# Score products in two column halves, then whole: two 64-column products become one of 128

## The chip, the core and the metric

The kernel runs on one core of a Trainium2 chip. The core has five engines that work through their own instruction queues and meet at semaphores: TensorE (PE, matrix products; its weight loads are listed apart as PEld), VectorE (DVE), ScalarE (ACT), GpSimd (POOL) and SyncE (SP, which here issues most DMAs). The metric is the device time of one execution in microseconds.

## What is computed

Thresholded attention over 8 batches of 8 heads, 576 positions and 64 numbers a head, followed by a gated MLP with a product over positions. Cut to what matters:

```python
scores = scale * np.matmul(q, k.transpose(0, 1, 3, 2))          # 576 x 576 for each head
thresh = np.max(scores, axis=-1, keepdims=True) - tau
scores = np.where(scores >= thresh, scores, -1000000000.0)
scores = scores - np.max(scores, axis=-1, keepdims=True)
attn = np.exp(scores)
attn = attn / (np.sum(attn, axis=-1, keepdims=True) + 1e-09)
x = np.matmul(attn, v)                                           # heads are then put side by side

h = np.maximum(x @ w_in, 0.0)
u, v = h[..., :512], h[..., 512:]
v_n = (v - mean(v)) / np.sqrt(var(v) + 1e-06)
v_s = np.einsum('ts,bsd->btd', w_spatial, v_n) + b_spatial[None, :, None]
out = (u * v_s) @ w_out
```

## The kernel before

Two heads are handled as a pair: head 0 of the pair lies in partitions 0 to 63 of a tile `qkT`, head 1 in 64 to 127, for q and for k, turned so that the 64 numbers of a head lie along the partitions. There are 32 pairs. The 576 rows of scores of a pair are cut into four chunks of 128 (c = 0 to 3) and a remainder of 64 rows; the remainders of two pairs that follow each other share a chunk of their own (c = 4). So every even pair has four steps and every odd pair five, 144 steps in all, 18 for each of the 8 batches. The list `steps` names the pair and the chunk of each step g.

A step computes the scores of 128 rows (for both heads, 576 columns each) in fp32 into one of two PSUM buffers, `s_ring[g % 2]`. A buffer spans three PSUM banks of 512 fp32 columns: head 0's scores start at column 96, head 1's at 864 (`at = (96, 864)`). Head 0 thus fills the rest of bank 0 (its first 416 columns, `cut`) and 160 columns of bank 1, head 1 fills 160 columns of bank 1 and 416 of bank 2. The two heads' products use different row halves of the array[...]. `part` (line 810) issues one stretch of columns of one head, as two products with 64 columns of weights each (k = 0 and 1), one for each half of the 128 score rows. In steps with c = 4 the two halves belong to two different pairs and so have different operands.

`scores` (line 823) issues three stretches: head 0's 160 columns in bank 1, head 1's 416 in bank 2, head 0's 416 in bank 0. `scores_end` (line 834) issues the last, head 1's 160 in bank 1. Both heads write bank 1 at different times, so `turn_bank` (line 829) puts an empty instruction on GpSimd, ScalarE or VectorE that waits for head 0's product in bank 1, and head 1's product waits for that.

After a step, `top` (line 840) takes the maximum over each head's 576 columns on VectorE (line 850), `shift` (line 856) makes the threshold's offset, ScalarE passes over each head (`spread`, lines 871 and 874), which frees the score buffer, and either ScalarE (`exps`, line 909) or VectorE (`keep` and `pick`, lines 893 and 902) turns the result into numerators. A DMA transposes them (`turn_p`, line 914), and TensorE multiplies them with v (lines 491 to 510). Two score buffers mean that step g + 2 begins once the passes of step g are done.

The order is written out by hand. For each batch a string of tokens is walked through, `S7:0` for `scores` of the batch's step 7, `G7`, `Y7` for `turn_bank` and `scores_end`, `M`, `B`, `E`, `F` for the maximum, the offset and the two passes, `Z`, `C`, `A` for the numerators, `T` for the transposing DMA, `P` for the product with v. Between them stand the tokens of the MLP (lines 627 to 767), the turning of q and k by TensorE (lines 434 and 453) and the loads (SyncE). Every engine works through its instructions in the order of this list. Between `S` and `Y` of one step no other TensorE work is listed as a rule, and nearly always other TensorE products, with weights of 128 by 128, lie between one step and the next.

The line numbers in the profile are those of the code printed here.

Of the kernel before, what the change touches and what calls it, by code (L numbers as in the profile page):

```python
# [184 lines left out]
def kernel(  # L185
# [18 lines left out]
    B, H, S, D = q.shape  # L204
# [5 lines left out]
    P = 128  # L210
# [15 lines left out]
    s_ring = [ps_s.tile([P, 1536], F32, name=f"s{i}") for i in range(2)]  # L226
# [147 lines left out]
    def shape_bias(_):  # L374


        for n in range(3):
            part = wsb[:, :, S + n]
            nc.gpsimd.tensor_copy(out=part, in_=bias)
            if n < 2:  # L380
                nc.gpsimd.tensor_tensor(out=bias, in0=bias, in1=part, op=ALU.subtract)
# [17 lines left out]
    qks, xns, xts = {}, {}, {}  # L399
# [86 lines left out]
    halves = [slice(64 * k, 64 * k + 64) for k in range(2)]  # L486
# [303 lines left out]
    at = (96, 864)  # L790
# [11 lines left out]
    def follow(b, a):  # L802

        tc.add_manual_dep(b.ins, a.ins.name, mybir.DependencyInfo(
            mybir.DependencyClass.Sync, mybir.DependencyReason.DATA), reason="shared bank")

    cut = 512 - at[0]
    opened, turned = {}, {}

    def part(g, h, lo, hi):  # L810

        i, c = steps[g]
        made = []
        for k in range(2):
            n, m = (i, 64 + c * P + 64 * k) if c < 4 else (i - 1 + k, S)
            made.append(nc.tensor.matmul(  # L816
                out=s_ring[g % 2][halves[k], at[h] + lo:at[h] + hi],
                lhsT=qks[n][halves[h], 0, m:m + 64],
                rhs=qks[n][halves[h], 1, 64 * (1 - h) + lo:64 * (1 - h) + hi],
                start=True, stop=True))  # L820
        return made

    def scores(g):

        opened[g] = part(g, 0, cut, S)[1]
        part(g, 1, S - cut, S)
        part(g, 0, 0, cut)

    def turn_bank(g, eng):

# [2 lines left out]

    def scores_end(g):

        follow(part(g, 1, 0, S - cut)[0], turned[g])

    negm = {}

# [255 lines left out]
    def run_token(tok, it):  # L1095
# [19 lines left out]
        m = 2 * b + a[0] if a else 0  # L1115
        if kind in "SGYMHKEFBZWCAT":
            {"S": scores, "G": lambda g: turn_bank(g, relay), "Y": scores_end, "M": top, "E": lambda g: spread(g, 0),
             "F": lambda g: spread(g, 1), "H": lambda g: top(g, slice(0, 1)),
             "K": lambda g: top(g, slice(1, 2)), "B": shift, "Z": exps, "W": mask, "C": keep, "A": pick, "T": turn_p}[kind](g)
# [124 lines left out]
```

## Time and profile before

| what | us |
|---|---|
| median of three runs (lowest to highest) | 434.66 (434.51 to 435.89) |
| the profiled execution's own time | 435.42 |
| its span, first to last instruction | 433.6 |
| score products, first to last start | 6.2 to 396.0 |
| MATMUL records of line 816 (two for each product) | 2304, 171.4 us busy |
| maximum, line 850 | 144 times 1.36 |
| passes of ScalarE, lines 871 and 874 | 288 times 0.74 |
| DMA | 88.15 MB, mean 203 GB/s |

The granted TensorE clock is full in every slice. A line of the timeline has the start, the length, the engine, the line of the code, the operation, the tile written and the tiles read, the shape of the array used by TensorE (rows*columns of weights, as in 64*64), the shape of one operand, how many instructions were merged, and in brackets the idle time before and what ended it. The starts of TensorE's records are observed, their ends are modelled.

### The profile page before, as it was taken

The page shows a single profiled execution, that of the slowest core. Times are in us where ns is not written, and L with a number is a line of the kernel's source. Part 1 is how long each engine was busy: PE and PEld are TensorE (multiplying, and loading weights), DVE is VectorE, ACT ScalarE, POOL GpSimd, SP SyncE. Part 2 cuts the span into 40 slices and gives each one's busy share as a digit, 9 for nine tenths or more (in the row PEclk, how much of TensorE's full clock was granted, in tenths as well). Part 3 has the DMA queues.
Part 4 walks back from the last instruction along what each step waited for, and adds up shares of the span by engine and source line. Part 5 has one row for each costly group of instructions (what it writes and reads, how often), then busy time and mean ns, then how long its engine had stood idle before and what let it go on. Part 6 is the DMA issues. An engine that isn't in the chain of part 4 may idle for free.

```text
span 433.6 us, 12917 instructions
## 1 busy us (share of the span) xinstructions
PE 407.3 (94%) x5028; PEld 253.7 (58%) x5028; DVE 374.6 (86%) x681; ACT 383.9 (89%) x587; POOL 167.5 (39%) x374
## 2 busy tenths in 40 slices
PE   7678879989999999998999999999999999999995
PEld 4446655565755666574665656555666656564642
DVE  6999989898989889987889988988999999998652
ACT  4999989999999988998988999999999989999262
POOL 1253525682335611545143713356114630264020
PEclk9999999999999999999999999999999999999999
DMA  7999999999899998999979999999999999889923
GB/s 195 224 237 232 246 247 221 194 212 197 226 241 212 246 208 183 218 184 178 254 139 250 216 159 248 233 209 205 232 209 232 181 232 194 172 124 193 164 68 118
DMA packets 224700, 88.15 MB, mean 203 GB/s; under 512 B 195648, under 2 KB 220352, under 8 KB 224640
## 3 DMA queue, kind: packets, MB, share of 16 engines
q1 hardware_dynamic: 224192, 86.75, 99.7%
q8 instruction: 39, 0.64, 0.6%
q10 hardware_dynamic: 368, 0.33, 0.2%
q0 software_dynamic: 80, 0.26, 0.2%
q14 instruction: 21, 0.17, 0.2%
HBM read 32.79 MB, written 9.44 MB: 97 GB/s over the span
## 4 chain that ended last, share of the span: by engine, by line
PE 64%; ACT 13%; DVE 8%; DMA 6%; issue 4%; POOL 3%; SPq 0%; ACTq 0%; DVEq 0%; POOLq 0%
PE s L816 26%; ACT e L874 6%; PE f L738 6%; DVE s L850 5%; PE f L496 5%; PE f L709 5%; PE f L434 4%; PE f L642 4%; PE f L767 4%; DMA pT<-p 3%; ACT p L909 2%; DMA xT<-xn 2%; ACT e L871 2%; PE f L491 2%; PE f L627 1%
## 5 line engine op out<-in xcount | busy, mean ns | idle before, releaser
L850 DVE TENSOR_REDUCE s<-s 128x2 f32<-128x1152 f32 x144 | 196.1, 1362 | 21.3 <-PE s L816 18.0
L816 PE MATMUL s<-qkT 64*64 64x160 f32 (+1 forms) x2304 | 171.4, 415 | 12.6 <-ACT e L874 6.6
L816 PEld LDWEIGHTS s<-qkT 64*64 64x64 f32 x2304 | 106.5, 131 | 71.3 <-ACT e L874 18.8
L874 ACT ACTIVATE e<-s,negm 128x576 f32<-128x576 f32 x192 | 133.1, 744 | 9.6 <-DVE negm L856 7.0
L909 ACT ACTIVATE p<-e 128x1152 f16<-128x1152 f32 x96 | 111.6, 1173 | 0.7 <-PE s L816 0.2
L871 ACT ACTIVATE e<-s,negm 128x576 f16<-128x576 f32 x96 | 66.8, 746 | 5.0 <-DVE negm L856 2.9
L320 POOL CAST v<-vl 128x512 bf16<-128x512 f32 x32 | 20.2, 631 | 77.0 <-PE s L816 65.7
L496 PE MATMUL f<-v,pT 128*128 128x65 bf16 x984 | 44.4, 194 | 0.0
L496 PEld LDWEIGHTS <-pT 128*128 128x128 f16 x1024 | 41.8, 98 | 2.2 <-issue 0.2
L293 POOL COPY qn<-ql 128x512 f32<-128x512 f32 x31 | 20.4, 659 | 49.9 <-PE s L816 47.5
L902 DVE TENSOR_TENSOR p<-e 128x576 int32<-128x576 int32 x48 | 37.2, 778 | 0.4 <-PE s L816 0.2
L738 PE MATMUL f<-wsT,vn 128*128 128x512 bf16 x135 | 33.0, 380 | 0.0
L491 PE MATMUL f<-v,pT 128*128 128x130 bf16 x123 | 27.3, 222 | 3.6 <-DMA pT<-p 3.5
L709 PE MATMUL f<-xT,w_in 128*128 128x512 bf16 x116 | 29.7, 380 | 0.5 <-ACT qkT L414 0.3
L694 POOL TENSOR_SCALAR vn<-vrel,rs,nm 128x512 bf16<-128x512 f32 (+1 forms) x35 | 28.1, 801 | 3.6
L642 PE MATMUL f<-w_in,xT 128*128 128x512 bf16 x112 | 27.9, 380 | 0.3 <-DMA xT<-xn 0.3
L446 POOL COPY qkT<-qkT 64x64 f32<-64x64 f32 x32 | 9.5, 296 | 44.8 <-PE s L816 17.6
L534 DVE TENSOR_TENSOR xn<-f,r 128x384 bf16<-128x384 f32 x46 | 24.9, 551 | 1.3 <-PE s L816 0.8
L856 DVE TENSOR_SCALAR negm<-s 128x2 f32<-128x2 f32 x144 | 22.2, 154 | 4.0 <-PE s L816 1.5
L767 PE MATMUL f<-w_o,gT 128*128 128x512 bf16 x100 | 25.4, 379 | 0.1
L893 DVE TENSOR_SCALAR e<-e 128x1152 uint16<-128x1152 f16 x48 | 23.0, 478 | 0.1
L687 POOL TENSOR_TENSOR rs<-rs,mhalf 128x1 f32<-128x1 f32 (+1 forms) x35 | 21.2, 607 | 2.9
(171 smaller groups left out, 531.4 us busy)
## 6 DMA issues: line engine op xcount, KB each, us to landing
vl<-in_v_dram SPq DMA_DIRECT2D x16, 512.0 KB, 5.3
ql<-in_q_dram SPq DMA_DIRECT2D x15, 512.0 KB, 4.6
kl<-in_k_dram SPq DMA_DIRECT2D x15, 512.0 KB, 5.3
out_dram<-oo SPq DMA_DIRECT2D x12, 512.0 KB, 3.7
pT<-p SPq DMA_TRANSPOSE x141, 4.6
uT<-in_moe_w_in_dram SPq DMA_DIRECT2D x3, 512.0 KB, 5.1
uT<-in_moe_w_spatial_dram SPq DMA_DIRECT2D x2, 576.0 KB, 4.4
vx<-in_v_dram SPq DMA_DIRECT2D x16, 64.0 KB, 4.3
```

The costliest lines, as they stand in the source:

```text
L491: nc.tensor.matmul(out=t[:, at:at + 130], lhsT=pt[:, 4, rows], rhs=vt[:, 4:6, :].rearrange("p b d -> p (b d)"), start=True, stop=False)
L496: nc.tensor.matmul(out=t[:, at + 65 * h:at + 65 * h + 65], lhsT=pt[:, 5 * h + j, rows], rhs=vt[:, 6 * h + j, :], start=False, stop=(h == 1 ...
L642: nc.tensor.matmul(out=t, lhsT=x_of(b, f, slice(c * P, (c + 1) * P)), rhs=w_in[:, f, 512:1024], start=(f == 0), stop=(f == 3))
L709: nc.tensor.matmul(out=t, lhsT=w_in[:, m, f * P:(f + 1) * P], rhs=x_of(b, m, slice(0, 512)), start=(m == 0), stop=(m == 3))
L738: nc.tensor.matmul(out=t, lhsT=vn[:, c, f * P:(f + 1) * P], rhs=wsT[:, c, 0:512], start=(c == 0), stop=(c == 4))
L767: nc.tensor.matmul(out=t[:n], lhsT=gs[b][:, f, c * P:c * P + n], rhs=w_o[:, f, :], start=(f == 0), stop=(f == 3))
L816: made.append(nc.tensor.matmul(out=s_ring[g % 2][halves[k], at[h] + lo:at[h] + hi], lhsT=qks[n][halves[h], 0, m:m + 64], rhs=qks[n][halves ...
L850: nc.vector.tensor_reduce(out=nm[:, heads], in_=view(s_ring[g % 2], at[h0], dims), axis=AX.X, op=ALU.max, negate=True)
L871: nc.scalar.activation(out=half_e(g)[0][:, S * h:S * h + S], in_=s, func=ACT.Exp, bias=bias_, scale=scale if steps[g][1] == 4 else 1.0)
L874: nc.scalar.activation(out=e, in_=s, func=ACT.Prelu, bias=bias_, scale=scale if steps[g][1] == 4 else 1.0, alpha=1e30)
L902: nc.vector.tensor_tensor(out=numerators(g).bitcast(I32), in0=e.bitcast(I32), in1=kept.bitcast(I32), op=ALU.bitwise_and)
L909: nc.scalar.activation(out=numerators(g), in_=e_ring[g % 3].rearrange("p h s -> p (h s)"), func=ACT.Exp)
```

## The change

`part` gets a flag `whole`. Where it is set and c < 4, one product with all 128 columns of weights (64 rows by 128 columns of the array) writes all 128 score rows, in place of two with 64 columns each. It is set for the second stretch of each head: head 0's 416 columns and head 1's last 160. The first stretch of each head, and all steps with c = 4, stay as they are.

```diff
-    def part(g, h, lo, hi):
+    def part(g, h, lo, hi, whole=False):
 
         i, c = steps[g]
+        whole = whole and c < 4
         made = []
-        for k in range(2):
+        for k in range(1 if whole else 2):
             n, m = (i, 64 + c * P + 64 * k) if c < 4 else (i - 1 + k, S)
             made.append(nc.tensor.matmul(
-                out=s_ring[g % 2][halves[k], at[h] + lo:at[h] + hi],
-                lhsT=qks[n][halves[h], 0, m:m + 64],
+                out=s_ring[g % 2][slice(0, P) if whole else halves[k], at[h] + lo:at[h] + hi],
+                lhsT=qks[n][halves[h], 0, m:m + (P if whole else 64)],
                 rhs=qks[n][halves[h], 1, 64 * (1 - h) + lo:64 * (1 - h) + hi],
                 start=True, stop=True))
         return made
...
-        part(g, 0, 0, cut)
+        part(g, 0, 0, cut, True)
...
-        follow(part(g, 1, 0, S - cut)[0], turned[g])
+        follow(part(g, 1, 0, S - cut, True)[0], turned[g])
```

## The prediction

> **What bounds the kernel now.** I began with the page: busy shares and the strip of 40 slices.
>
> ```profile
> PE 407.3 (94%) x5028; PEld 253.7 (58%) x5028; DVE 374.6 (86%) x681; ACT 383.9 (89%) x587; POOL 167.5 (39%) x374
> ...
> PE   7678879989999999998999999999999999999995
> ...
> PE 64%; ACT 13%; DVE 8%; DMA 6%; issue 4%; POOL 3%; SPq 0%; ACTq 0%; DVEq 0%; POOLq 0%
> PE s L816 26%; ACT e L874 6%; PE f L738 6%; DVE s L850 5%; PE f L496 5%; PE f L709 5%; PE f L434 4%; PE f L642 4%; PE f L767 4%; DMA pT<-p 3%; ACT p L909 2%; DMA xT<-xn 2%; ACT e L871 2%; PE f L491 2%; PE f L627 1%
> ```
>
> TensorE carries 64% of the chain of waits, and line 816, the one that is changed, 26% alone. Because a share is a mean over stages, I cut the span by stage (columns: stretch, its length, then PE, PEld, DVE, ACT, POOL busy):
>
> ```profile
> 6.20:100.00 93.80, 78.66 (x1049) 52.07 (x1052) 84.68 (x141) 87.01 (x130) 45.41 (x93) 1.00 1.13 228
> 100.00:397.00 297.00, 292.53 (x3650) 182.65 (x3647) 266.52 (x471) 278.07 (x424) 117.86 (x269) 1.00 1.04 205
> ```
>
> From 100 to 397 us PE lacks only 4.5 us of being always busy: what PE loses there, the kernel loses. From 6.2 to 100 it sits idle for 15.1 us, and the chain there runs through other engines too: 12.23 PE, 13.56 DVE, 15.22 ACT, and again. All 144 score steps lie in these two stretches; 38 begin before 100 us, 106 after. (DMA shows 9 in nearly every slice, a second full resource, but one that only gains room if the rest is slower.)
>
> **One step as it is.** The timeline around one step, then two pieces of the chain in order of time:
>
> ```profile
> 204.37 0.60 PE L434 MATMUL f<-identf,kn 128*128 128x128 f32 x4
> 204.90 0.91 PEld L816 LDWEIGHTS s<-qkT 64*64 64x64 f32 x16 [0.17 <-issue]
> 204.90 1.20 PE L816 MATMUL s<-qkT 64*64 64x160 f32 x16
> 206.03 0.14 PEld L453 LDWEIGHTS f<-identf,rl 128*128 128x128 f32 x1 [0.23 <-ACT qkT L416]
> 206.03 0.33 PE L453 MATMUL f<-identf,rl 128*128 128x128 f32 x1
> ```
>
> ```profile
> 204.97 1.13 PE s L816 x12
> ...
> 361.02 2.10 PE s L816 x24
> ```
>
> A step costs PE 1.13 us from its first weight load to the next work's. What is in it comes from the forms of line 816 (busy, mean ns):
>
> ```profile
> L816 PE MATMUL s<-qkT 64*64 64x416 f32 x1152 | 167.8, 521 | 0.0
> L816 PE MATMUL s<-qkT 64*64 64x160 f32 x1152 | 132.1, 308 | 12.6 <-ACT e L874 6.6 <-ACT e L871 3.9 <-DVE negm L856 1.5
> ```
>
> Each product is two records. 521 - 308 = 213 ns for 256 columns more is 0.83 ns a column, so 416 columns stream in 346 ns and 160 in 133; the rest of a record (shortest 296, less 133) is 163 ns of tail. Head 0 uses the upper 64 rows of the array, head 1 the lower 64, and they run side by side: head 0 streams 160 then 416, head 1 416 then 160. Each half needs 2 x 133 + 2 x 346 = 958 ns. Single records show it: from the step's start, head 1's second 416 record starts at 0.42 us, but head 0's 416 already at 0.325, in the array's other half. 0.96 plus about 0.05 exposed load plus the tail's part that the next work waits for makes 1.13.
>
> **What a change of shape costs.** Before the step runs a 128*128 shape. PE L434 ends at 204.97 by the record, and the first 64*64 load starts at 204.90, 0.07 before that end. Inside one shape loads go far ahead:
>
> ```profile
> 208.50 0.66 PE L434 MATMUL f<-identf,qn 128*128 128x128 f32 x4
> 208.89 0.64 PEld L709 LDWEIGHTS <-w_in 128*128 128x128 bf16 x4
> ...
> 244.27 0.41 PE L496 MATMUL f<-v,pT 128*128 128x65 bf16 x8
> 244.62 0.11 PEld L504 LDWEIGHTS <-pT 128*64 128x64 f16 x2
> ```
>
> L709 loads 0.27 us before L434's end (both 128*128); L504, where only the columns change (128*128 to 128*64), again waits until 0.06 before it. I went through the single records of all 301 changes of shape in this trace, of six kinds (128*128, 128*64, 64*64, each to each other): the earliest load is 0.073 us before the modelled end of the last product, never earlier; and in the 65 changes whose load waits for no semaphore it is 0.071 or 0.072 each time, never later. So a change of shape by itself makes the load wait until the array is empty. Price: after a 160-column record the next load starts 0.224 us after that record's start, and 0.05 more of load is exposed (first records 348 ns against 296), where 0.133 would do within a shape: 0.224 + 0.052 - 0.133 = **0.14 us**.
>
> **The change, part by part.**
>
> *Removed:* in steps with c < 4 the second pair of products becomes two instead of four. c = 4 occurs once in every odd pair, 16 of 144 steps; 128 steps change, and 128 x 4 = 512 records of each kind go (5028 to 4516). They streamed beside each other, so this frees no streaming time: 128 columns of weights take the same 0.83 ns per moving column. Line 434's fp32 records with 128*128 say so: 273 ns for 128 columns is 107 plus 166. At most the few ns between twin records go, 6.5 ns a step, 0.8 us in all.
>
> *Added:* a change of shape inside the step, 64*64 to 64*128. No row has it. Lower bound: nothing, if the upper half simply goes on. Upper bound, by the rows above: the whole array empties. I take the upper one, since all six kinds of change do that. The Trainium skill speaks against this change too: "TensorEngine Tiling (Array Packing)", Key Properties, says that changing the tiling mode, unlike changing the tile, drains TensorE. The page has no price; the trace has. Then, from the step's start: head 1's second 416 record starts at 0.42 and ends at 0.42 + 0.51 = 0.93; the first 64*128 load may start at 0.93 - 0.07 = 0.86. Head 0's 416 columns, which began at 0.325, begin now: second record at 0.86 + 0.05 + 0.35 = 1.26, end 1.26 + 0.51 = 1.77, next shape's load at 1.70. Head 1's 160 run beside it and end by 1.36. **1.70 - 1.13 = 0.57 us a step.** The same from the parts: 2 x 346 + 2 x 346 streamed one after the other is 1384 in place of 958, 0.43, plus one change at 0.14.
>
> Here a second rule could matter. "TensorE: Matmul & The Clock Gate", LDWEIGHTS, prices a weight load by its columns, 1/1.2 ns each, so 128 columns load 53 ns longer than 64, which the emptied array would expose: 128 x 0.053 = 6.8 us more. The row says less: after a change, line 453's fp32 load of 128 columns lengthens its product from 273 to 328 ns, 55, against 52 for 64 columns. I take the row (0.4 us in all) and keep 6.8 for the top of the range.
>
> 128 x 0.57 = 73 us. Seven steps start 0.77 to 1.1 us after the step before, overlapping it (the 2.10 us for two above, against 2 x 1.13): now 64*128 to 64*64 lies between and stops that, 7 x 0.16 = 1.1. Sum **74 us of PE work**.
>
> *Moved:* the relay (line 831), an empty instruction on POOL, ACT or DVE that tells head 1's last product that head 0 has left the shared bank, still waits for the same 64*64 product, ending at 0.49 after the step's start. Its follower could go at 0.61 before and at 0.86 now, so 0.25 us of cover come on top; that costs nothing. The DVE maximum (1.36), and behind it ACT's two passes (1.38), start 0.57 later; from 100 us on they had waited in PE's shadow, DVE 30 and ACT 19 us idle, and get more room. No DMA is issued or moved.
>
> *What absorbs it:* PE's idle, 15.1 + 4.5 = 19.6 us at most. From 8 to 35 us the chain goes PE 1.25, DVE 1.38, ACT 1.38 around the two score buffers, 4.4 us for two steps, so only every second step's 0.57 is on it: some six of twelve are hidden, 3.4 us. Of the 8.2 us idle between 30 and 100, and of the 4.5 after, I take half: 4 and 2. About 10 in all (chosen; ends 0 and 19.6).
>
> Sum against the profiled execution: 435.42 (span 433.6 plus 1.8 around it) + 74 - 10 = 499. That run lies 0.76 above the median of the three shown, 434.66; from the median **498 us**.
>
> **The rivals.**
>
> *Only the changed half waits (8%).* 64*128 over the upper rows might wait for head 0 alone. Its last 160 record starts at 0.195, so its load comes at 0.195 + 0.224 = 0.42 and its columns stream from 0.47 in place of 0.325, and the step ends 0.14 later: 128 x 0.14 = 18, a third absorbed, 447 us. For: no change in this trace leaves an untouched half running, so none shows what happens to it. Against: the page says the engine drains, and every record here waits for the last product of all.
>
> *The halves stop running side by side in 64*128 (5%).* Then head 1's 2 x 133 come after head 0: 128 x 0.27 = 34 more, 532 us. For: no 64*128 row. Against: 64*64 halves overlap fully.
>
> *No drain, no loss (5%).* Row split unchanged, so 64*128 could follow at 0.325 as now; half as many loads in that part, 0.8 us gained, 434 us, not slower. It decides if the change costs under about 0.01 us a step (128 x 0.01 = 1.3 us, which 0.3% of the time is). Against: the column-only change at 244.62.
>
> *It does not take effect (under 1%):* the new flag reaches `slice(0, P)` for every c < 4.
>
> **How the numbers follow.** Array emptied: 82%. Its own range is 434.66 + 74 - 20 = 489 to 434.66 + 74 + 6.8 = 515. The other cases lie far from it and are left out; I round the range to 485 to 515, with room below for a step that is 0.03 us cheaper than worked out. 0.3%, 1.3 us, is about what can be told from no change. Slower holds the first three cases, 95%; the no-loss case splits into 2% same and 3% faster.
>
> **What would show it.** Line 816 with 512 records 64*128; in a step, the first 64*128 load some 0.86 us after the first 64*64 load and 0.07 before the recorded end of head 1's 416; pieces of 1.70 in place of 1.13 in the chain; PE near always busy from 35 us on; DVE and ACT shares down by a tenth. A first 64*128 load at 0.42 or 0.19 would make it wrong, as would head 1's 160 beginning after head 0's 416.

## The result, and the profile after

The kernel after takes 1.149 times as long as the kernel before (95% interval 1.143 to 1.155). Its median of six runs is 504.79 us against 435.5 us for the kernel before beside it; three of the six ran longer than the rest (508 to 518 us), and this ratio, like those below, leaves such runs out; the other three took 500.35, 500.43 and 501.5 us. The profiled execution took 500.43 us, with a span of 498.7.

From the page of the kernel after, busy time, the strip for TensorE and the chain that ended last:

```profile
PE 481.9 (97%) x4469; PEld 224.1 (45%) x4516; DVE 377.6 (76%) x681; ACT 392.2 (79%) x587; POOL 165.5 (33%) x374
...
PE   8789999999999999999999999999999999999996
...
PE 87%; ACT 6%; DVE 3%; issue 2%; DMA 1%; SPq 0%; ACTq 0%; DVEq 0%
PE s L817 45%; PE f L496 6%; PE f L434 5%; PE f L738 5%; PE f L642 5%; PE f L709 4%; PE f L767 4%; ACT e L875 3%; DVE s L851 2%; PE f L491 2%; PE f L627 2%; PE f L453 1%; ACT p L910 1%; ACT e L872 1%; PE t L940 1%
```

The load records of TensorE went from 5028 to 4516 (of the matmul records some 50 are missing here), and yet PE is busy for 75 us longer. The score products, now line 817, hold 45% of the chain, where they held 26%. DVE and ACT have the same work as before in a longer span, so their shares fell from 86% to 76% and from 89% to 79%.

One step in the timeline of the loads, and the same step and what follows it in the chain in order of time:

```profile
252.61 0.21 PEld L817 LDWEIGHTS s<-qkT 64*64 64x64 f32 x8 [0.17 <-issue]
253.47 0.30 PEld L817 LDWEIGHTS s<-qkT 64*128 64x128 f32 x4 [0.65 <-issue]
254.36 0.14 PEld L453 LDWEIGHTS f<-identf,rl 128*128 128x128 f32 x1 [0.59 <-issue]
```

```profile
252.68 1.75 PE s L817 x9
254.44 0.26 PE f L453
```

The first 64*128 load comes 253.47 - 252.61 = 0.86 us after the first load of the step, and no semaphore is named for its wait ("issue"). The next work's load comes 1.75 us after the step's start, where it was 1.13. In the single records, all 128 changes from 64*64 to 64*128 have the load 0.071 to 0.073 us before the recorded end of head 1's 416 columns, the last product of all, and none of the 128 waits for a semaphore.

The loads of line 817 by form (busy, mean ns, idle before):

```profile
L817 PEld LDWEIGHTS s<-qkT 64*64 64x64 f32 x1280 | 38.7, 131 | 46.3 <-issue 12.2 <-ACT e L875 10.7 <-ACT e L872 6.0
L817 PEld LDWEIGHTS s<-qkT 64*128 64x128 f32 x512 | 38.6, 184 | 83.4 <-issue 83.4
```

A load of 128 columns takes 184 ns where one of 64 takes 131. The 83.4 us of idle ahead of the 128-column loads are the 128 waits for the emptied array, 0.65 each. ("Emptied" is a reading: the ends of records are modelled, but the starts are observed, and by them each of these loads comes 0.44 us after the start of a 416-column record, which streams for 0.35.)

By stage (length, then PE, PEld, DVE, ACT, POOL busy):

```profile
6.20:100.00 93.80, 87.17 (x808) 39.28 (x810) 76.01 (x125) 78.62 (x118) 38.09 (x80) 1.00 0.97 211
100.00:459.00 359.00, 355.58 (x3320) 164.79 (x3358) 276.71 (x484) 292.40 (x435) 122.14 (x282) 1.00 0.84 174
```

PE's idle in the first 100 us fell from 15.1 to 6.6 us, though that stretch now holds fewer steps. In the long stretch PE lacks 3.4 of 359 us.

### The profile page after: what moved, and what is told of

Its sections match the earlier page's. It is cut to its first block, busy times and chain, and to the rows that moved or that the text cites. A ratio compares the mean times of both kernels' runs of the same rounds, so it can differ in the third digit from the quotient of the medians.

```text
span 498.7 us, 11846 instructions
## 1 busy us (share of the span) xinstructions
PE 481.9 (97%) x4469; PEld 224.1 (45%) x4516; DVE 377.6 (76%) x681; ACT 392.2 (79%) x587; POOL 165.5 (33%) x374
## 4 chain that ended last, share of the span: by engine, by line
PE 87%; ACT 6%; DVE 3%; issue 2%; DMA 1%; SPq 0%; ACTq 0%; DVEq 0%
PE s L817 45%; PE f L496 6%; PE f L434 5%; PE f L738 5%; PE f L642 5%; PE f L709 4%; PE f L767 4%; ACT e L875 3%; DVE s L851 2%; PE f L491 2%; PE f L627 2%; PE f L453 1%; ACT p L910 1%; ACT e L872 1%; PE t L940 1%
## 5 line engine op out<-in xcount | busy, mean ns | idle before, releaser
L817 PE MATMUL s<-qkT 64*64 64x160 f32 (+3 forms) x1792 | 251.3, 433 | 7.3 <-ACT e L875 4.3
L875 ACT ACTIVATE e<-s,negm 128x576 f32<-128x576 f32 x192 | 132.6, 739 | 21.1 <-DVE negm L857 17.6
L817 PEld LDWEIGHTS s<-qkT 64*64 64x64 f32 (+1 forms) x1792 | 77.3, 146 | 129.7 <-issue 95.6
L416 ACT COPY qkT<-f 128x512 f32<-128x512 f32 (+1 forms) x44 | 19.3, 439 | 17.1 <-PE f L453 10.2
L694 POOL TENSOR_SCALAR vn<-vrel,rs,nm 128x512 bf16<-128x512 f32 (+1 forms) x35 | 26.8, 767 | 3.5
```

The costliest lines, as they stand in the source:

```text
L817: made.append(nc.tensor.matmul(out=s_ring[g % 2][slice(0, P) if whole else halves[k], at[h] + lo:at[h] + hi], lhsT=qks[n][halves[h], 0, m: ...
L875: nc.scalar.activation(out=e, in_=s, func=ACT.Prelu, bias=bias_, scale=scale if steps[g][1] == 4 else 1.0, alpha=1e30)
```

## The experiments

The theory: going from one array shape to another inside a step makes the next load wait until all products are done, so that two parts that ran beside each other run one after the other. The first rival: products with 128 columns of weights are slow in themselves. The second: the array empties only in one direction of the change. The short diffs are against the kernel after, save the last one.

**No change of shape inside the step.** All four stretches with c < 4 use 128 columns.

```diff
-        opened[g] = part(g, 0, cut, S)[1]
-        part(g, 1, S - cut, S)
+        opened[g] = part(g, 0, cut, S, True)[-1]
+        part(g, 1, S - cut, S, True)
```

> All four stretches of a changed step use 128 columns of weights, so no change of shape lies inside a step. Theory (the array empties at a change of shape): a step goes back from 1.75 us to 1.17 or 1.18, the 0.05 above the step of the kernel before being the longer first weight load; 128 x 0.045 = 6 us less what PE's idle absorbs, so 436 to 442 us. Rival (128-column products are slow in themselves, in twice as many places here): a step of 1.75 us or more, 500 us or more.

Measured: ratio 1.0108 (1.0059 to 1.0157), median 437.78 us against 433.91. From its chain in order of time:

```profile
204.06 1.17 PE s L817 x6
205.23 0.26 PE f L453
```

A step of 1.17 us although every product has 128 columns: heads 0 and 1 do run side by side in 64*128, and the width of the products is not what costs. The first rival falls. What remains, 1.17 against 1.13, fits the longer first load (184 against 131 ns), and the kernel with 64-column halves everywhere stays the fastest, by 1%.

**One change of shape, late.** Only head 1's last 160 columns use 128 columns.

```diff
-        part(g, 0, 0, cut, True)
+        part(g, 0, 0, cut)
```

> Only head 1's last 160 columns are one product of 128 columns; head 0's 416 are again two of 64. One change of shape in the step, but after both halves have done their 416 columns. Theory: the 64*128 load comes 1.12 us after the step's start, the step lasts 1.58 us, 0.45 more than before; 128 x 0.45 = 58 us less 10 to 15, so 472 to 489 us. Rival (cost goes with the columns streamed by 128-column products): 160 of 576 columns, 28% of the 65 us, so about 453 us.

Measured: ratio 1.1058 (1.0997 to 1.1119), median 480.37 us. Its chain:

```profile
223.56 1.58 PE s L817 x12
225.15 0.26 PE f L453
```

1.58 us, as worked out, for 160 columns in a new shape. The timeline shows the load 224.61 - 223.49 = 1.12 us after the step's start. It is put down to the relay on POOL there, but that relay ended at 224.05, 0.56 us before the load. In the single records all 128 such loads come 0.071 or 0.072 us before the last recorded end, one fixed distance each time, which is the emptied array's mark and not the relay's:

```profile
223.49 0.47 PEld L817 LDWEIGHTS s<-qkT 64*64 64x64 f32 x12 [0.17 <-ACT p L910]
224.61 0.29 PEld L817 LDWEIGHTS s<-qkT 64*128 64x128 f32 x2 [0.65 <-POOLq L832]
```

**Two changes of shape.** Only head 0's 416 columns use 128 columns, and head 1's last 160 return to 64.

```diff
-        follow(part(g, 1, 0, S - cut, True)[0], turned[g])
+        follow(part(g, 1, 0, S - cut)[0], turned[g])
```

> Only head 0's 416 columns are one product of 128 columns; head 1's last 160 are again two of 64. Two changes of shape in the step. Theory: three parts one after the other, next load 2.17 us after the step's start, 1.04 more than before; 128 x 1.04 = 133 us less 15 or so, 540 to 560 us, dearer than the whole change although it has half its 128-column products. Rival (cost goes with the columns streamed by 128-column products): 416 of 576, 72% of 65 us, about 482 us.

Measured first: 564.79 and 574.26 us. In the profile the steps form 131 groups (one step, or two with no other TensorE work between them); 107 last 2.17 us, but early on four groups of two steps last 7.80 us and one 6.86. That was more than the step explains, so it ran once more:

> The variant with only head 0's 416 columns as one product of 128 columns once more, because in its first profile five stretches of two steps between 17 and 61 us took 7.8 us where two steps of 2.17 make 4.34, and both its times hold something that the step's length doesn't explain. Theory: all steps with c < 4 at 2.17 us; added 128 x 1.04 + 1 = 134 us less 10 to 17 that PE's idle absorbs, so 551 to 558 us. Rival (a further cost comes with two changes of shape, outside of the step): 565 us again.

Measured: 551.21 us in the profiled execution and 551.0 in another, against 435.31 for the kernel before; two more, with a mean granted clock of 0.969 and 0.962, took 564.3 and 566.89. Timeline of the loads in the profiled one:

```profile
254.69 0.21 PEld L817 LDWEIGHTS s<-qkT 64*64 64x64 f32 x8 [0.42 <-ACT uT L412]
255.55 0.29 PEld L817 LDWEIGHTS s<-qkT 64*128 64x128 f32 x2 [0.65 <-issue]
256.44 0.19 PEld L817 LDWEIGHTS s<-qkT 64*64 64x64 f32 x4 [0.60 <-issue]
256.86 0.76 PEld L738 LDWEIGHTS <-vn 128*128 128x128 bf16 x5 [0.23 <-issue]
```

Three parts, each beginning when the one before is done: 0.86, 0.89, 0.42, together 2.17. Half of the change's 128-column products cost 116 us where the whole change costs 65. The longer groups didn't return, so a further cost outside of the step is not supported. The trace of the first run points to the clock instead. The same form of record from 6.2 to 62 us, then from 70 us on:

```profile
L817 PE MATMUL s<-qkT 64*64 64x416 f32 x56 | 21.8, 915 | 0.0
L817 PE MATMUL s<-qkT 64*64 64x416 f32 x572 | 120.8, 531 | 0.0
```

Single second records took 897 ns for 416 columns and 471 for 160 until 66 us, and 509 and 296 from 68 us on: 1.66 ns a column, then 0.83. That trace has no record of the clock before 68.4 us, and the full clock that its page shows there is no measurement. The next variant's has one, and there records of the same 897 and 471 ns stand where the granted clock is 0.50. The other run of the first pair, 564.79 us, had a mean granted clock of 0.965.

**The shapes in the other order.** First stretches with 128 columns, second ones with 64.

```diff
-        opened[g] = part(g, 0, cut, S)[1]
-        part(g, 1, S - cut, S)
-        part(g, 0, 0, cut, True)
+        opened[g] = part(g, 0, cut, S, True)[-1]
+        part(g, 1, S - cut, S, True)
+        part(g, 0, 0, cut)
...
-        follow(part(g, 1, 0, S - cut, True)[0], turned[g])
+        follow(part(g, 1, 0, S - cut)[0], turned[g])
```

> The order of shapes is turned round: the first stretch of each head uses 128 columns, the second two products of 64. One change of shape in the step, at the same place, in the other direction. Theory: 1.74 us a step and 496 to 506 us, as the change itself. Rival (only going over to the wider shape empties the array): the second stretch of head 0 would start at about 0.38 us, the step would last 1.2 us, 437 to 445 us.

Measured: 500.61 and 511.52 us in two runs, which gives no interval; the verdict rests on the step. The longer run is the profiled one; from 20 to 50 us (busy PE, PEld, DVE, ACT, POOL, then the granted clock) it shows

```profile
20.00:50.00 30.00, 30.00 (x127) 10.92 (x128) 15.09 (x23) 17.65 (x26) 8.17 (x23) 0.50 0.67 146
```

and from 60 us to the last score step a granted clock of 1.00. The loads of a step there:

```profile
234.17 0.30 PEld L817 LDWEIGHTS s<-qkT 64*128 64x128 f32 x4 [0.17 <-issue]
235.07 0.21 PEld L817 LDWEIGHTS s<-qkT 64*64 64x64 f32 x8 [0.60 <-issue]
235.92 0.14 PEld L453 LDWEIGHTS f<-identf,rl 128*128 128x128 f32 x1 [0.64 <-issue]
```

0.90 and then 0.85, 1.75 in all. In the single records all 128 loads that follow this change come 0.071 or 0.072 us before the last recorded end, and none waits for a semaphore. Going to the narrower shape empties the array as well; the second rival falls.

**Where the added work is hidden.** The change in the first 38 steps alone, and in the others alone (`g < 38`, or `g >= 38`):

```diff
-        whole = whole and c < 4
+        whole = whole and c < 4 and g < 38
```

> The change in steps 0 to 37 alone, those that begin before 100 us, 34 of them with c < 4. Their added PE work is 34 x 0.62 = 21 us. Theory (the idle of PE before 100 us hides it, since there the chain runs through DVE and ACT as well): 9 to 12 us of it are hidden, 9 to 12 us are seen, a ratio of 1.021 to 1.028. Rival (what is hidden is spread evenly over all changed steps, 14 us of 80 in the whole change): 17 us are seen, a ratio of 1.04.

> The change in steps 38 to 143 alone, 94 of them with c < 4, after 100 us. Their added PE work is 94 x 0.62 + 1 = 59 us. Theory (PE has only 4.5 us of idle there): 3 to 5 us are hidden, 54 to 57 us are seen, a ratio of 1.125 to 1.13. Rival (hidden evenly, 17% of it): 49 us are seen, a ratio of 1.113.

Measured: early 1.0289 (1.0233 to 1.0345), late 1.1225 (1.1184 to 1.1265). In us, by the kernel before beside them at 435.57: 12.6 and 53.4 seen. The early value lies just past the upper end expected, the late one just under the lower end; each interval reaches the theory's range and excludes the rival's value. Hidden are then 21.1 - 12.6 = 8.5 of the early work, 40%, and 58.7 - 53.4 = 5.3 of the late, 9% (94 x 0.621, and 0.3 for pairs of steps that no longer overlap). The stretch that holds the early steps, then the late one, from the windows of the two kernels:

```profile
6.20:112.00 105.80, 98.73 (x920) 44.76 (x923) 85.99 (x144) 89.29 (x131) 44.90 (x95) 1.00 0.97 206
```

```profile
100.00:450.00 350.00, 346.90 (x3233) 160.59 (x3271) 269.24 (x470) 285.29 (x424) 116.63 (x269) 1.00 0.83 175
```

Early idle of PE went from 15.1 to 7.1 us, which is nearly all of the 8.5. Late idle went only from 4.5 to 3.1. In the single records the time between the score steps (from the load that follows a step to the first load of the next) adds up to 223.7 us in the kernel before and 217.2 here, 6.5 less, so the rest was hidden between the steps as well. That these are waits covered in the record by the modelled tail of the product before is an inference and was not tried.

**What a load of 128 fp32 columns costs.** In the kernel before, the 31 turnings of line 453 become plain products.

```diff
-            nc.tensor.transpose(out=t[:, 0:P], in_=nat_rest(i), identity=identf)
+            nc.tensor.matmul(out=t[:, 0:P], lhsT=nat_rest(i), rhs=identf, start=True, stop=True)
```

> The kernel before, with the 31 turnings of line 453 written as a plain fp32 product with the identity in place of the transposing form: same 128*128 shape, same 128 columns of fp32 weights, two records in place of one. Theory (a plain fp32 load costs by its columns and the transposing one is a quicker load): the load record grows from 0.14 to about 0.18 us and the first record, where it follows a score step, from 0.33 to about 0.38 us, as in the 64*128 products. Rival (the longer load comes from using 64 of the 128 rows): load 0.14 and first record 0.33 stay. The time: 31 x 0.16 = 5 us at most over the kernel before.

Measured: one time of 439.24 us against 435.57, and from the instructions of that line (shortest, median, longest in ns):

```profile
L453 PEld LDWEIGHTS f<-identf,rl x62: 186/189/192, 9.9 to 382.9; 128*128 128x128 f32 x62
L453 PE MATMUL f<-identf,rl x62: 272/275/377, 10.0 to 383.0; 128*128 128x128 f32 x62
```

The same line in the kernel before:

```profile
L453 PEld LDWEIGHTS f<-identf,rl x31: 138/139/143, 9.9 to 379.2; 128*128 128x128 f32 x31
L453 PE MATMUL f<-identf,rl x31: 272/328/333, 10.0 to 379.2; 128*128 128x128 f32 x31
```

The array shape and the 128 columns are the same; only the transposing form is gone, and the load grows from 139 to 189 ns. After a change of shape the product's record is 377, 104 over the 273 of an unexposed one, where the transposing one was 328, 55 over. The 64*128 products show the same 104: their first records are 0.40 and 0.61 us where their second ones are 0.296 and 0.51. The one uses 128 rows of the array and the other 64, so the number of rows is not what makes the load longer.

## Why the prediction was right, and where it was off

- **TensorE bounds the kernel, and line 816 most of all.** Held. Nearly every us added to the steps after 100 us showed.
- **The unpriced change of shape.** Taken at its upper bound, that the whole array empties. Held to the hundredth: the load comes 0.86 us after the step's start in 124 of 128 cases (1.01 to 1.06 in the four that overlap the step before), and 0.07 before the recorded end in all 128. The Trainium skill's rule that weighed against the change ("TensorEngine Tiling (Array Packing)", Key Properties) agrees with the trace of the kernel after in all pairs of shapes that occur in it, in either direction: of 436 changes none has a load more than 0.073 us before the recorded end.
- **1.70 us a step.** Measured 1.75. The term that was mis-sized is the exposed load: the prediction took line 453's 55 ns over the rule of "TensorE: Matmul & The Clock Gate" on loads. The row was a transposing load, which is not the same thing. The rule's 53 ns more than for 64 columns was right: 104 against 52 is 52 more. Over 128 steps that is 6.7 us, nearly all of the 6.8 kept for the top of the range.
- **The seven overlapping pairs, 1.1 us.** Mis-sized, but small. In five of them the first step has c = 4, so that 64*64 follows 64*64 and nothing stops the overlap: four last 2.72 us, 0.16 less than 1.13 + 1.75, and the fifth holds a wait for a semaphore (3.00 us). The other two lost the overlap (3.50 us, twice 1.75), which is 0.3 us.
- **About 10 us hidden.** 128 x 0.621 (1.752 - 1.131 in the records) + 0.3 = 79.8 us were added and the span grew by 498.7 - 433.6 = 65.1, so 14.7 were hidden: mis-sized by 5, though within the 0 to 19.6 that it was chosen from. The half-hidden early stretch held: its chain still goes PE, DVE, ACT, one score step for every two (14.09 to 19.14 in the kernel after, 5.05 us, where it was 4.41).
- **The sum.** 499 us for the profiled execution, 500.43 measured. The two misses, 6 us too little added (6.7 of loads, less 0.8 of pairs) and 5 too little hidden, nearly cancel. That the total came so close is luck; what the prediction had right is what happens in a step.
- **Relay, maximum, passes.** Head 1's first 64*128 load came 0.006 to 0.008 us after head 0's in all 128 steps. The relay was not late, and the DVE and ACT work kept its length.
- **The rivals.** "Only the changed half waits" fell with the load at 0.86 instead of 0.42; "halves no longer side by side" with the all-128 kernel's 1.17; "no drain" with both.

## What to carry to other kernels

Inside a group of small products that share the array in tiles, as here, keep one tile shape. The price of mixing shapes is not the 0.14 us of the emptied array alone but the overlap lost across the change (0.43 us in the change itself, three times as much), and it depends on where the change stands and grows with each one: one early 0.62, one late 0.45, two 1.04 us a step. Before a longer stretch is put down to the code, compare the time of one record of the same form: where all of them are longer, it can be the clock. When a load is priced by a row of the trace, take a row of the same form of instruction: a transposing load of the same size is no stand-in for a plain one.

## What the runs showed that was not expected

The exposed part of a transposing fp32 load of 128 columns is 55 ns, that of a plain one 104, in the same 128*128 shape. And a wait for an empty array can be put down to a semaphore: in the variant with one late change, 59.3 us of waits are listed against the relay on POOL, although every one of these loads came at the fixed 0.07 us before the last product's recorded end, in the step shown 0.56 us after the relay was done.
